# Chunked attention before two feed-forward stages: paired units in two-bank accumulators, a five-step weight conversion, and a reordered prologue

## The chip, the cores and the metric

The kernel runs on one core of one Trainium2 chip. The metric is the device time of one execution in microseconds (us); lower is better. The core has five engines, each with its own queue of instructions that it works in order: TensorE (PE in the profile, and PEld for its loads of stationary operands), VectorE (DVE), ScalarE (ACT), GpSimd (POOL) and SyncE (SP), which here only starts DMA transfers. PE writes to eight banks of PSUM; DVE and ACT read them.

## What is computed

```python
# attention: 4 batches x 8 heads, 768 positions, 64 per head; chunks of 32 queries
k_full = concat(mem_k (8), k[c_start-16 : c_end+8])      # 64 keys per chunk
a = exp(scale * (q_c @ k_full.T) - max); a = a / (sum(a) + 1e-9)
x = a @ v_full                                            # -> 3072 rows of 512
# first feed-forward stage
h = x @ w_in            # 512 x 2048
y = (relu(h) ** 2) @ w_out                                # 2048 x 512
# second stage: one of 8 experts per row, chosen by argmax(y @ w_gate)
out = gate * sigmoid(y @ w_output_gate)[e] * (relu(y @ w1[e]) @ w2[e])
```

All arrays are float32, and the result has to keep that precision.

## The kernel before

**Precision.** Most products use a 4-byte format that keeps fewer bits than float32, so each operand is split into a high part and a low part (the rest), and each product is made three times: high x high, low x high, high x low. Attention and transposes use plain float32 products. The weights of the first stage are stored as float64 (two 32-bit words per number), and are converted on the chip, tile by tile. There are 16 tiles of 1024 columns, i0, o0, i1, o1, ... (i for `w_in`, o for `w_out`). One tile takes an ACT operation that rescales the exponent (line 240, `split_w_exp`), a shift and two operations that put in the low word and the sign on DVE (lines 246 to 248, `split_w_bits`), the high part on ACT (line 260) and the low part on DVE (line 261, both in `split_w_end`). The raw tiles share three buffers (`kvp`).

**Attention.** A unit is 128 rows of one batch; there are 24, and two make a block of 256 rows. Four head pairs (`hp`) and four chunks (`c`) lie in a unit. The keys and values are laid out block-diagonally, 128 x 128 for two heads, with zeros off the diagonal, so that one product serves two heads:

```python
for hp in range(4):                      # products, lines 126-131
    for c in range(4):
        rows = slice(32 * c, 32 * c + 32)
        nc.tensor.matmul(ps[rows, hp, :], lhsT=left[:, hp, rows], rhs=right[:, hp, c, :], ...)
```

Each of these 16 products appears as two instructions in the trace. The steps of a unit are: scores on PE (`pss`), the maximum and the subtraction on DVE, exp on ACT, sum and reciprocal on DVE (`norm`), a transpose on PE (`psa`) and its copy on ACT (`at`), the product with the values on PE (`psx`), the scaling on DVE (line 196), a transpose on PE (`pst`), its high part on ACT (line 217) and its low part on DVE (line 218). For units 0 to 3 keys and values come compact and are spread over zeroed tiles by copies on DVE, ACT and GpSimd (`spread`, line 124); later units load the zeros with them (1 MB for keys, 1 MB for values).

**First stage.** For each block and each of 16 slices `f` of 128 hidden columns there is one step: `mm1` (12 products into `ph`, line 297), `relu` (r, g, gh and gl on ACT and DVE, lines 307 to 316), and `mm2` of two steps earlier (6 products into `py`, lines 326 to 328). Blocks 0 and 1 go side by side, as the weight tiles become ready; the others one after another.

**Gate and experts.** When a block's rows are done, the gate transposes them (`gate_transpose`), computes logits, chooses an expert (`gate_choose`) and counts positions (`gate_rank`), and GpSimd writes the row's number to its expert's list. Afterwards rows are gathered by expert, two tiles of 128 at a time (`Pair`) and then one at a time (`Slot`), with the expert's weights split on the way (line 564).

**What sets the order.** Instructions are issued in the order in which the program writes them. The prologue (lines 844 to 953) is written out by hand, with dummy products on PE (`keep_busy`). After it, `seq` lists the steps, n = 4, 5, ..., and `plan(n, fn)` hangs other work on a step: it comes after that step's `mm1` and before its `mm2`. Weight tile m must be ready by step 2m. `plan_unit` (line 729) places the parts of a unit, `plan_gate` (line 761) those of a gate; their comments are numbers of steps only. Unit work and gate work use the accumulators `ps_a`: two tiles of one bank each; `ps_y` holds four of one bank, `ps_h` two.

Of the kernel before, what the change touches and what calls it, by code (L numbers as in the profile page):

```python
# [8 lines left out]
F32 = mybir.dt.float32  # L9
# [8 lines left out]
P = 128  # L18
NT = 3072
D = 512  # L20
# [12 lines left out]
NCOMP = 4  # L33
SPIN = (6, 4, 3)
# [12 lines left out]
SPARE_KV = [("i6", "o6"), ("i7", "o7")]  # L47
# [3 lines left out]
def chunk_attention_relu2_moe_top1_kernel(ctx: ExitStack, tc, qt, kvc, kw, vw, w_in, w_out, wg, wexp, consts, out):  # L51
# [14 lines left out]
    ps_y = ctx.enter_context(tc.tile_pool(name="ps_y", bufs=4, space=bass.MemoryType.PSUM))  # L66
    ps_a = ctx.enter_context(tc.tile_pool(name="ps_a", bufs=2, space=bass.MemoryType.PSUM))
# [20 lines left out]
    class Unit:  # L88
        def __init__(self, u):
            self.u = u  # L90
            self.b, self.j = divmod(u, UPS)

        def load_qk(self):
            u = self.u
            self.q = qp.tile([P, 4, P], F32, tag="q", name=f"q{u}")
            nc.sync.dma_start(self.q, qt[u])
            if u < NCOMP:
                self.k, self.v = diag[u % 2]
                self.load_compact(0)
            else:  # L100
                self.k = kvp.tile([P, 4, 4, P], F32, tag="kv", name=f"k{u}")
                nc.sync.dma_start(self.k, kw[u - NCOMP])

        def load_v(self):
            u = self.u
            if u < NCOMP:
                self.load_compact(1)
            else:
                self.v = kvp.tile([P, 4, 4, P], F32, tag="kv", name=f"v{u}")
                nc.sync.dma_start(self.v, vw[u - NCOMP])  # L110


        def load_compact(self, w):
            u = self.u
            if w == 0:
                self.c = wpool.tile([P, 2, 4, 4, 64], F32, tag=SPARE_C[u], name=f"c{u}")
            nc.sync.dma_start(self.c[:, w], kvc[u, :, w])

        def spread(self, w, *copies):
            t = self.v if w else self.k  # L120
            for n, copy in enumerate(copies):
                if copy is not None:
                    rows = slice(64 * n, 64 * n + 64)
                    copy(t[rows, :, :, 64 * n : 64 * n + 64], self.c[rows, w])

        def products(self, ps, left, right):

            for hp in range(4):
                for c in range(4):
                    rows = slice(32 * c, 32 * c + 32)  # L130
                    nc.tensor.matmul(ps[rows, hp, :], lhsT=left[:, hp, rows], rhs=right[:, hp, c, :], start=True, stop=True)
# [7 lines left out]
        def scores_mm(self, pool=ps_a, tag="a"):  # L139
            self.ps = pool.tile([P, 4, P], F32, tag=tag, name=f"pss{self.u}")  # L140
            self.products(self.ps, self.q, self.k)

        def scores_max(self):
            u = self.u
            self.sc = self.ps.rearrange("p a (b k) -> p (a b) k", k=64)
            self.mx = sp_.tile([P, 8], F32, tag="mx", name=f"mx{u}")
            nc.vector.tensor_reduce(out=self.mx, in_=self.sc, axis=AX.X, op=ALU.max)

        def scores_sub(self):
            u = self.u  # L150
            self.e = ap_.tile([P, 8, 64], F32, tag="e", name=f"e{u}")
            nc.vector.tensor_tensor(
                self.e, self.sc, self.mx.unsqueeze(2).to_broadcast([P, 8, 64]), op=ALU.subtract
            )
            if self.j == 0:
                nc.vector.memset(self.e[0:32, :, 8:24], -BIG)
            if self.j == UPS - 1:
                nc.vector.memset(self.e[96:128, :, 56:64], -BIG)

        def scores_exp(self):  # L160
            nc.scalar.activation(self.e, self.e, ACTF.Exp, scale=0.125)

        def norm(self):
            u = self.u
            sm = sp_.tile([P, 8], F32, tag="sm", name=f"sm{u}")
            nc.vector.tensor_reduce(out=sm, in_=self.e, axis=AX.X, op=ALU.add)
            nc.vector.tensor_scalar_add(sm, sm, EPS)
            self.r = sp_.tile([P, 8], F32, tag="rs", name=f"rs{u}")
            nc.vector.reciprocal(self.r, sm)
# [5 lines left out]
        def transpose_a_mm(self):  # L175
            self.ps = ps_a.tile([P, 4, P], F32, tag="a", name=f"psa{self.u}")
            ef = self.e.rearrange("p a k -> p (a k)")
            for hp in range(4):
                nc.tensor.transpose(self.ps[:, hp, :], ef[:, hp * P : hp * P + P], ident)

        def transpose_a_copy(self):
            self.at = ap_.tile([P, 4, P], F32, tag="at", name=f"at{self.u}")
            nc.scalar.copy(self.at, self.ps)
# [5 lines left out]
        def av_mm(self):  # L189
            self.ps = ps_a.tile([P, 4, P], F32, tag="a", name=f"psx{self.u}")  # L190
            self.products(self.ps, self.at, self.v)
# [914 lines left out]
```

## Time and profile before

| | before |
|---|---|
| median of 3 runs | 1022.12 us (1020.71 to 1026.53) |
| the profiled execution | 1022.48 us |
| its span, first to last instruction | 1020.7 us |
| mean granted PE clock | 0.988 of full speed |
| DMA moved | 149.97 MB, mean 147 GB/s |

The span is 1.8 us shorter than the execution's own time, which has some work around it. "Busy" is time in which at least one instruction of an engine runs; instructions on PE overlap, so their durations add up to more than the busy time, and the distance from one start to the next tells what one costs. In the rows, `out<-in` names the tiles written and read without their numbers, `x32` is a count, and what stands in brackets is the idle time before the instruction with what ended it. A clock of 1.00 is PE's level of 2.4 GHz, one of 0.50 its level of 1.2 GHz.

### The profile page before, as it was taken

To read this page: it belongs to the slowest core of one execution; us is meant where nothing else is said; L and a number is where in the kernel's file an instruction comes from. 1 tells how busy PE (TensorE), PEld (TensorE's weight loads), DVE (VectorE), ACT (ScalarE), POOL (GpSimd) and SP (SyncE) were. 2 spreads that over 40 slices of the span, in tenths; PEclk is the share of its full clock that TensorE was granted. 3 is DMA by queue.
4 is the path that set the end of the run, shared out by engine and by line. 5 is a ranking of instruction groups with operands and counts; after the bars stand their busy time and mean duration, and the time that the engine had idled before them with its cause. 6 is when DMAs were issued, how large, how long until landed. Compare 5 with 4: busy or idle time off the path is not lost. (4 is left out here: it accounts for less than half of the span.)

```text
span 1020.7 us, 18715 instructions
## 1 busy us (share of the span) xinstructions
PE 985.6 (97%) x7421; PEld 866.9 (85%) x7421; DVE 620.7 (61%) x1232; ACT 470.7 (46%) x873; POOL 103.7 (10%) x99
## 2 busy tenths in 40 slices
PE   6789999999999999999999999989899999999997
PEld 3678888889898988989898989878799999888886
DVE  5799855454444545454545453566586666789995
ACT  4668533333333333333233333254344544688885
POOL 3000000000000000000000000010211222121111
PEclk9799999999999999999999999999899999999999
DMA  9256654261323223242423200094776655465531
GB/s 333 91 192 220 238 173 159 43 159 48 122 87 114 94 79 129 73 135 73 134 74 101 95 4 21 7 382 170 220 290 228 233 213 202 161 227 190 207 117 39
DMA packets 34733, 149.97 MB, mean 147 GB/s; under 512 B 8975, under 2 KB 9487, under 8 KB 20562
## 3 DMA queue, kind: packets, MB, share of 16 engines
q1 hardware_dynamic: 29394, 134.81, 38.2%
q0 software_dynamic: 5248, 13.92, 4.1%
q8 instruction: 60, 0.98, 0.4%
q14 instruction: 31, 0.25, 0.1%
HBM read 163.16 MB, written 13.61 MB: 173 GB/s over the span
## 5 line engine op out<-in xcount | busy, mean ns | idle before, releaser
L297 PE MATMUL ph<-xh,wi 128*128 128x256 f32 x1536 | 286.4, 284 | 5.6 <-DVE wi L261 2.6
L297 PEld LDWEIGHTS ph<-xh,wi 128*128 128x128 f32 x1536 | 252.5, 191 | 23.5 <-DVE wi L261 3.2
L297 PE MATMUL ph<-xl,wi 128*128 128x256 f32 x768 | 218.0, 284 | 0.1
L312 DVE TENSOR_TENSOR g<-r 128x256 f32<-128x256 f32 x168 | 71.1, 423 | 234.3 <-ACT r L307 233.8
L307 ACT ACTIVATE r<-ph 128x256 f32<-128x256 f32 x192 | 73.4, 382 | 300.1 <-PE ph L297 296.2
L326 PE MATMUL py<-wo,gh 128*128 128x512 f32 x384 | 161.5, 420 | 1.4 <-ACT wo L260 1.4
L327 PE MATMUL py<-wo,gh 128*128 128x512 f32 x384 | 151.9, 396 | 0.8 <-DVE wo L261 0.8
L328 PE MATMUL py<-wo,gl 128*128 128x512 f32 x384 | 151.4, 394 | 1.1 <-DVE gl L316 1.1
L297 PEld LDWEIGHTS ph<-xl,wi 128*128 128x128 f32 x768 | 147.0, 191 | 0.5 <-DVE xl L218 0.5
L564 DVE TENSOR_TENSOR x<-raw,x 128x1024 fp32r<-128x1024 f32 x88 | 103.1, 1221 | 8.9 <-ACT x L563 8.7
L316 DVE TENSOR_TENSOR gl<-g,gh 128x256 fp32r<-128x256 f32 x192 | 81.5, 425 | 24.1 <-ACT gh L314 1.7
L564 DVE TENSOR_TENSOR p<-raw,p 128x1024 fp32r<-128x1024 f32 x64 | 78.1, 1222 | 27.8 <-ACT p L563 27.7
L421 POOL DMA_INDIRECT listd<-ent,idx x24 | 25.5, 1060 | 643.5 <-DVE idx L419 555.2
L328 PEld LDWEIGHTS py<-wo,gl 128*128 128x128 f32 x384 | 72.4, 189 | 19.9 <-DVE gl L316 3.2
L563 ACT CAST x<-raw 128x1024 fp32r<-128x1024 f32 x88 | 87.3, 1055 | 0.0
L326 PEld LDWEIGHTS py<-wo,gh 128*128 128x128 f32 x384 | 72.6, 189 | 16.8 <-issue 4.8
L314 ACT ACTIVATE gh<-r 128x256 fp32r<-128x256 f32 x192 | 79.8, 415 | 5.3
L327 PEld LDWEIGHTS py<-wo,gh 128*128 128x128 f32 x384 | 73.0, 190 | 9.5 <-DVE wo L261 1.1
L563 ACT CAST p<-raw 128x1024 fp32r<-128x1024 f32 x64 | 66.6, 1042 | 6.5 <-DMA raw<-in_wexp 6.5
L705 PE MATMUL po<-x,ht 128*128 128x512 f32 x264 | 65.1, 397 | 0.0
L705 PEld LDWEIGHTS po<-x,ht 128*128 128x128 f32 x264 | 48.2, 188 | 9.2
L578 POOL DMA_INDIRECT out<-o,slots x27 | 33.9, 1256 | 208.8 <-ACT o L574 90.9
(227 smaller groups left out, 1439.5 us busy)
## 6 DMA issues: line engine op xcount, KB each, us to landing
raw<-in_wexp SPq DMA_DIRECT2D x82, 1024.0 KB
k<-in_kw SPq DMA_DIRECT2D x20, 1024.0 KB
v<-in_vw SPq DMA_DIRECT2D x20, 1024.0 KB
raw_i<-in_w_in SPq DMA_DIRECT2D x7, 1024.0 KB
raw_o<-in_w_out SPq DMA_DIRECT2D x7, 1024.0 KB
q<-in_qt SPq DMA_DIRECT2D x24, 256.0 KB
ydram<-y SPq DMA_DIRECT2D x24, 256.0 KB
c<-in_kvc SPq DMA_DIRECT2D x8, 512.0 KB
```

The costliest lines, as they stand in the source:

```text
L297: nc.tensor.matmul(ph, lhsT=w_in_part(w, f, k), rhs=x[:, k, :], start=(n == 0), stop=(n == 11))
L307: nc.scalar.activation(r, ph, ACTF.Relu, scale=WSCALE)
L312: nc.vector.tensor_tensor(g, r, r, op=ALU.mult)
L314: nc.scalar.activation(gh, r, ACTF.Square)
L316: nc.vector.tensor_tensor(gl, g, gh.bitcast(F32), op=ALU.subtract)
L326: nc.tensor.matmul(self.y[t], lhsT=gh[:, s], rhs=w_out_part(wh, f), start=(f == 0), stop=False)
L327: nc.tensor.matmul(self.y[t], lhsT=gh[:, s], rhs=w_out_part(wl, f), start=False, stop=False)
L328: nc.tensor.matmul(self.y[t], lhsT=gl[:, s], rhs=w_out_part(wh, f), start=False, stop=(f == NF - 1))
L563: nc.scalar.copy(w[:, 0], t)
L564: nc.vector.tensor_tensor(w[:, 1], t, w[:, 0].bitcast(F32), op=ALU.subtract)
L578: nc.gpsimd.indirect_dma_start(out=out, out_offset=bass.IndirectOffsetOnAxis(ap=slots[:, c, 0:1].bitcast(U32), axis=0), in_=self.y[t], in_ ...
L705: nc.tensor.matmul(self.po, lhsT=self.ht[:, part, f, :], rhs=w[:, wp, j * D : j * D + D], start=(f == 0 and part == 0 and wp == 0), stop=( ...
```

## The change

- **Products in row halves.** Keys and values are no longer block-diagonal. Each head is multiplied by itself: 64 rows (one half of the array), 64 columns, into one of two banks by the head's parity. All units load keys and values compact, 1 MB for both.
- **Pairs of units.** `Duo` replaces `Unit`: from block 1 on each of the steps above is made once for the two units of a block, on tiles of 1024 columns and accumulators of two banks. Block 0's units go singly in the prologue. `e`, `at` and `x` have one buffer each instead of two.
- **Accumulators.** `ps_a` is one tile of two banks, `ps_y` two of two banks. A gate's two transposes become one step, and so do a pair's; a slot's two transposes `psh` share one tile.
- **Weight conversion.** `split_w_bits` and `split_w_end` become five parts (exp, shift, or, high, low) with steps of their own, so that the exp and shift of the next tile stand ahead of the low part of this one. In the prologue only i0 is converted in halves.
- **Loads.** Queries and keys of units 0 to 3 come in one load each (rows of 6 KB), and the values of two units in one. A one-element copy on GpSimd (`hold`) into a tile makes the loads behind it wait: those of block 1 for block 0's first maximum, o0 for a reciprocal.
- **Dummies.** 41 dummy products in nine places instead of 25 in four.
- **Plan.** New steps for everything named; gates of blocks 0 to 9 come later.

```diff
-    ps_y = ... tile_pool(name="ps_y", bufs=4, space=PSUM)
-    ps_a = ... tile_pool(name="ps_a", bufs=2, space=PSUM)
+    ps_y = ... tile_pool(name="ps_y", bufs=2, space=PSUM)
+    ps_a = ... tile_pool(name="ps_a", bufs=1, space=PSUM)
...
+        def products(self, left, right, ts):
+            for i, t in enumerate(ts):
+                for hp in range(4):
+                    for par in range(2):
+                        half = slice(64 * par, 64 * par + 64)
+                        for c in range(4):
+                            rows = slice(32 * c, 32 * c + 32)
+                            n = 64 * (4 * i + hp)
+                            nc.tensor.matmul(
+                                self.ps[ts][rows, par, n : n + 64],
+                                lhsT=left[t][half, hp, rows],
+                                rhs=right[t][half, hp, c, :], start=True, stop=True)
+        def banks(self, name, ts, pool, tag):
+            self.ps[ts] = pool.tile([P, TPB, D], F32, tag=tag, ...)
...
-    plan(4, split_w_end, *tiles[3])
-    for m in range(4, 16):
-        n = 4 + (m - 4) * 3 // 2
-        plan(n, split_w, *tiles[m])
-        plan(n + 2, split_w_end, *tiles[m])
-        if m + 3 < 16:
-            plan(n, load_w, *tiles[m + 3])
+    bits = dict(zip(range(3, 16), (2, 4, 6, 8, 10, 12, 14, 15, 17, 18, 20, 21, 23)))
+    for m, n in bits.items():
+        if m > 4:
+            plan(bits[m - 1], split_w_exp, *tiles[m])
+            plan(bits[m - 1] + 1, split_w_shift, *tiles[m])
+        if m > 3:
+            plan(n, split_w_or, *tiles[m])
+            plan(n + 1, split_w_hi, *tiles[m])
+            plan(n + 1, split_w_lo, *tiles[m])
+        if m > 6:
+            plan(bits[m - 3] + 1, load_w, *tiles[m])
...
-        plan_unit(2 * b, n + 1, n + 4, n + 5, n + 7)
-        plan_unit(2 * b + 1, n + 6, n + 9, n + 10, n + 12)
+        plan_duo(b, n + 1, n + 3, n + 4, n + 6)
...
-        plan_gate(b, at[b, NF - 1] + (5, 11, 4)[min(b, 2)])
+        plan_gate(b, at[b, NF - 1] + (10, 12, 9)[min(b, 2)])
...
-        plan(last + 13 + t, pairs[0].transpose, t)
+    plan(last + 13, pairs[0].transpose)
...
-            plan(n + 5 + t, after.transpose, t)
+        plan(n + 5, after.transpose)
...
+        d0.load_first_qk(0); d0.load_first_qk(1); (ident); load_w(*i0, halves=a); d0.load_first_v()
+        keep_busy(12)
+        d0.scores_mm(u0)
+        keep_busy(4)
+        d0.scores_max(u0)
+        hold(d1.first[0], d0.mx[u0][0:1, 0, 0:1])
+        d1.load_first_qk(0); d1.load_first_qk(1); load_w(*i0, halves=b); d1.load_first_v()
+        d0.scores_sub(u0); d0.scores_mm(u1, *other); d0.scores_exp(u0); split_w_exp(*i0, a)
+        d0.transpose_a_mm(u0); d0.transpose_a_copy(u0); keep_busy(3)
+        d0.scores_max(u1); d0.scores_sub(u1); d0.scores_exp(u1); d0.norm(u0)
+        split_w_shift(*i0, a); split_w_or(*i0, a, steps=(0,))
+        d0.av_mm(u0); d0.av_scale(u0); d0.transpose_a_mm(u1, *other); d0.transpose_a_copy(u1); keep_busy(3)
+        d0.norm(u1); hold(o0t, d0.r[u1]); load_w(*o0); load_w(*i1); (consts)
...
+        d1.scores_mm(); split_w_exp(*i0, b); b0.mm1_products(0); keep_busy(8)
+        d1.scores_max(); d1.scores_sub(); b0.relu(0); d1.scores_exp()
+        split_w_shift(*i0, b); split_w_or(*i0, b); ...; split_w_lo(*i0, b); keep_busy(3)
+        d1.av_mm(); split_w_exp(*o0); b0.mm1_products(1); d1.av_scale()
+        split_w_shift(*o0); split_w_or(*o0, steps=(0,)); d1.transpose_x_mm(); d1.transpose_x_hi()
+        b0.relu(1); keep_busy(4); d1.transpose_x_lo(); split_w_or(*o0, steps=(1,))
+        b1.mm1_products(0); load_w(*o1); split_w_exp(*i1); split_w_hi(*o0); split_w_shift(*i1); split_w_lo(*o0)
+        b1.relu(0); split_w_or(*i1); load_w(*i2); b1.mm1_products(1); split_w_exp(*o1); b1.relu(1)
+        split_w_hi(*i1); split_w_shift(*o1); split_w_lo(*i1); b0.mm2(0); split_w_or(*o1)
+        load_w(*o2); split_w_exp(*i2); b0.mm2(1); split_w_hi(*o1); split_w_shift(*i2); split_w_lo(*o1)
```

(Lines of the prologue are joined with semicolons here.) The pair's gate, `Block.mm2`, `Pair.mm2` and `Slot` take their accumulators in tiles of two banks, and `yt` uses the tag of the converted weights; what they compute is unchanged.

## Rows read from the trace of the kernel before

**Rows 1.** The page: busy us, share of the span and instructions of each engine.

```profile
PE 985.6 (97%) x7421; PEld 866.9 (85%) x7421; DVE 620.7 (61%) x1232; ACT 470.7 (46%) x873; POOL 103.7 (10%) x99
```

**Rows 2.** Windows: each engine's busy us and instructions, PE clock, DMA share, GB/s.

```profile
5.00:68.70 63.70, 45.40 (x439) 35.07 (x436) 46.49 (x76) 37.89 (x63) 6.63 (x10) 0.87 0.57 208
68.70:117.00 48.30, 47.22 (x294) 41.32 (x295) 47.61 (x57) 37.97 (x68) 0.00 (x0) 1.00 0.65 232
150.00:640.00 490.00, 490.00 (x4231) 438.54 (x4230) 231.97 (x645) 159.33 (x390) 20.50 (x20) 1.00 0.29 91
```

**Rows 3.** Timeline of PE at 300 us: start, duration, line, operation, count.

```profile
302.46 0.40 PE L297 MATMUL ph<-xh,wi 128*128 128x256 f32 x2
...
305.28 0.40 PE L297 MATMUL ph<-xh,wi 128*128 128x256 f32 x2
...
310.92 0.40 PE L297 MATMUL ph<-xh,wi 128*128 128x256 f32 x2
...
314.96 0.40 PE L297 MATMUL ph<-xh,wi 128*128 128x256 f32 x2
```

**Rows 4.** Timeline of PE, prologue: sets of 32 small products.

```profile
13.99 1.94 PE L131 MATMUL pss<-diag_i,q 128*32 128x128 f32 x32
15.70 1.18 PE L131 MATMUL psx<-diag_o,at 128*32 128x128 f32 x32
...
19.89 1.08 PE L131 MATMUL psx<-diag_o,at 128*32 128x128 f32 x32
20.79 1.06 PE L131 MATMUL pss<-diag_i,q 128*32 128x128 f32 x32
```

**Rows 5.** Window of one such set; the clock stands third last.

```profile
13.99:15.70 1.71, 1.71 (x34) 1.59 (x36) 0.00 (x0) 1.58 (x3) 0.66 (x1) 0.50 1.02 407
```

**Rows 6.** Timelines of ACT, DVE and PE, prologue.

```profile
5.58 1.04 ACT L124 COPY diag_i<-c 64x1024 f32<-64x1024 f32 x1 [3.54 <-DMA c<-in_kvc]
...
7.82 0.69 DVE L147 TENSOR_REDUCE mx<-pss 128x8 f32<-128x512 f32 x1 [1.49 <-PE pss L131]
...
68.69 0.39 PE L297 MATMUL ph<-xh,wi 128*128 128x256 f32 x1 [2.30 <-DVE wi L261]
```

**Rows 7.** Groups on DVE, 5 to 68.7 us: busy us, mean ns, idle before.

```profile
L316 DVE TENSOR_TENSOR gl<-g,gh 128x256 fp32r<-128x256 f32 x8 | 3.4, 421 | 1.7 <-ACT gh L314 1.7
...
L147 DVE TENSOR_REDUCE mx<-pss 128x8 f32<-128x512 f32 x4 | 2.7, 684 | 5.6 <-PE pss L131 5.6
...
L124 DVE COPY diag_i<-c 64x1024 f32<-64x1024 f32 x3 | 2.1, 705 | 4.2 <-DMA c<-in_kvc 4.2
L246 DVE TENSOR_SCALAR ws_i<-ws_i 128x512 int32<-128x512 int32 x4 | 1.7, 418 | 0.0
...
L248 DVE SCALAR_TENSOR_TENSOR ws_o<-raw_o,ws_o 128x1024 int32<-128x1024 int32 x2 | 2.5, 1225 | 0.1
...
L246 DVE TENSOR_SCALAR ws_o<-ws_o 128x1024 int32<-128x1024 int32 x2 | 1.4, 692 | 0.3 <-ACT ws_o L240 0.3
```

**Rows 8.** Windows of the first 15 us; the last two columns are DMA.

```profile
0.00:5.00 5.00, 3.99 (x10) 1.49 (x11) 1.82 (x2) 1.28 (x1) 4.29 (x10) 1.00 0.57 170
5.00:10.00 5.00, 3.57 (x42) 1.47 (x39) 2.30 (x4) 2.36 (x3) 2.18 (x2) 1.00 0.94 326
10.00:15.00 5.00, 2.05 (x24) 1.66 (x28) 0.69 (x1) 3.34 (x5) 1.03 (x1) 0.75 0.99 348
```

**Rows 9.** Groups on DVE, whole span: one operation of a block's rank.

```profile
L415 DVE TENSOR_TENSOR pb<-psr,base 128x8 f32<-128x8 f32 x24 | 3.9, 162 | 0.4
```

**Rows 10.** Timelines of GpSimd and PE: gathers and the first gathered rows.

```profile
665.25 0.97 POOL L542 DMA_INDIRECT ys<-ydram,slots  x1 [7.51 <-PE py L328]
666.53 0.96 POOL L542 DMA_INDIRECT ys<-ydram,slots  x1 [0.30 <-issue]
...
672.95 0.63 PE L553 MATMUL psz<-cst,ys 128*128 128x128 f32 x4 [3.20 <-DMA ys<-ydram,slots]
...
726.79 1.08 PE L553 MATMUL psz<-cst,ys 128*128 128x128 f32 x4 [4.31 <-DMA ys<-ydram,slots]
```

More of the change, by code (lines that the diff above doesn't have):

```diff
@@ L32 @@
 BIG = 1.0e30
-NCOMP = 4
-SPIN = (6, 4, 3)
+EARLY = 4
+BOTH = (0, 1)
 F2B = F2 // P
@@ L85, in chunk_attention_relu2_moe_top1_kernel @@
     wh, wl = {}, {}
[L88 to L131, printed above, removed]
@@ L137, in scores, with scores_mm @@
             self.scores_exp()
[L139 to L151, printed above, removed]
+        def scores_mm(self, ts=BOTH, pool=ps_a, tag="a"):
+            self.banks("pss", ts, pool, tag)
+            self.products(self.q, self.k, ts)
@@ L155, in scores_sub @@
[L155 to L166, printed above, removed]
+                self.e[:, self.heads(ts)].rearrange("p a b k -> p b a k"),
@@ L226, in load_w @@
         t = raw[kind, g].rearrange("p n two -> p (n two)")
+        if not issue:
+            return t
         src = (w_in if kind == "i" else w_out)[g].bitcast(I32)
@@ L321, in mm2 @@
             if f == 0:
-                self.y = [ps_y.tile([P, D], F32, tag="y", name=f"py{b}_{t}") for t in range(TPB)]
+                y = ps_y.tile([P, TPB, D], F32, tag="y", name=f"py{b}")
+                self.y = [y[:, t] for t in range(TPB)]
             gh, gl = self.g.pop(f)
@@ L624, in mm2 @@
             if f == 0:
-                self.po = [ps_y.tile([P, D], F32, tag="y", name=f"po{p}_{t}") for t in range(TPB)]
+                po = ps_y.tile([P, TPB, D], F32, tag="y", name=f"po{p}")
+                self.po = [po[:, t] for t in range(TPB)]
             gh, gl = self.g.pop(f)
@@ L713, in chunk_attention_relu2_moe_top1_kernel @@
     tiles = [(kind, g) for g in range(8) for kind in "io"]
-    units = {u: Unit(u) for u in range(NU)}
+    duos = {b: Duo(b) for b in range(NB)}
     blocks = {b: Block(b) for b in range(NB)}
@@ new lines, in chunk_attention_relu2_moe_top1_kernel @@
+        d0.norm(u0)
+        split_w_shift(*i0, a)
+        split_w_or(*i0, a, steps=(0,))
+        d0.av_mm(u0)
+        d0.av_scale(u0)
+        d0.transpose_a_mm(u1, *other)
+        d0.transpose_a_copy(u1)
+        keep_busy(3)
+        d0.norm(u1)
+        o0t = load_w(*o0, issue=False)
+        hold(o0t.bitcast(F32), d0.r[u1][0:1, 0, 0:1])
+        load_w(*o0)
+        load_w(*i1)
+        nc.sync.dma_start(cst[:, P:], consts[:, P:])
+        d0.av_mm(u1, *other)
+        d0.av_scale(u1)
```

482 lines of the change are left out of this document (267 added, 215 removed).

## The prediction

> **What bounds the kernel now.** I read the page's busy line first [rows 1]: TensorE (PE) is busy for 97% of the span, VectorE (DVE) for 61%. An average over the span hides stages, so the table of windows comes next [rows 2]. From 150 to 640 us PE is busy for all 490 us at full clock, while DVE works 232 us: there only work taken off PE shortens the time. From 5.0 to 68.7 us it is the other way: PE works 45.4 of 63.7 us, DVE 46.5, and DVE waits for 17.2 us. There a chain through all engines sets the end. From 68.7 to 117 us both are nearly full (47.2 and 47.6 of 48.3 us).
>
> The timeline of PE shows what attention costs in the full stage [rows 3]. A plain step of the planner (12 products of the first matmul, 6 of the second) lasts 305.28 - 302.46 = 2.82 us. The step into which the scores of one unit are put lasts 314.96 - 310.92 = 4.04 us. So one unit's set of 32 small products costs 1.22 us of PE time. Where two such sets stand back to back [rows 4], the second starts 20.79 - 19.89 = 0.90 us after the first: 0.90 us is the products, 28 ns each, and 1.22 - 0.90 = 0.32 us is paid for entering and leaving. At a granted clock of 0.50 the same 32 products take 15.70 - 13.99 = 1.71 us [rows 4, 5], nearly twice as long: their price follows TensorE's clock.
>
> The prologue's timeline has three marks [rows 6]: at 5.58 us DVE may begin to spread the first keys, at 7.82 it takes the first maximum, and at 68.69 PE goes on in step 8 after 2.30 us of waiting for DVE's last operation on weight tile i2. From there PE hardly waits.
>
> **The change, part by part.**
>
> *Products in halves.* The products no longer multiply through zeros. Each 128-row, 128-column product becomes two of 64 rows and 64 columns, on the two row halves of the array, with outputs in two banks; two units are done in one set. A set has 128 instructions instead of 2 x 32 = 64, and 24 units become 12 pairs. Ten pairs (blocks 2 to 11) lie in or beside the full stage, with two sets each: 20 places. Before, a place costs 2 x 1.22 = 2.44 us. After, entering and leaving is paid once (0.32), and the products lie between two bounds. Below: half the columns and twice the tiles at work, so a quarter of 28 ns each: 128 x 7 = 0.90 us, in all 1.22. Above: each instruction costs what one costs now: 128 x 28 = 3.6, in all 3.9. In between: columns set the price, but the two halves of rows don't run at once: 128 x 14 = 1.8, in all 2.1. The trace speaks for columns: the price nearly doubled with the half clock [rows 4, 5], and four column tiles now run side by side. I take the lower end plus 0.2 us for a sequencer that must now issue four times as fast: 1.42 us. 20 x (2.44 - 1.42) = **20 us less**; ends 24 less and 30 more.
>
> A page of the Trainium skill speaks against this: "TensorE: Matmul & The Clock Gate", section "Back-to-back issue gap", gives a product of 1 to 64 columns a floor of about 25 ns. By it a place would cost about 3.5 us, some 1.1 more than now. No row of this trace has products this narrow in a long set, so neither is shown.
>
> *Prologue.* I count DVE's work up to i2's end, since DVE is what step 8 waits for. Before: 46.5 us between 5.0 and 68.7 [rows 2]. Gone are four spreading copies (4 x 0.7: 2.8 us) [rows 7]. Units 2 and 3 are paired: five operations of 1024 elements (about 1.22) for ten of 512 (0.69): 0.8 less. Tiles o0 and i1 are converted whole, not in halves: for each 0.42 + 3 x 0.69 twice is 5.0, against 0.69 + 3 x 1.22 = 4.4: together 1.2 less. Of tile o2 only the shift (0.69) still stands ahead of i2's end, not all three bit operations (3.1): 2.4 less. That leaves 46.5 - 7.2 = 39.3 us.
>
> When can it start? The first queries and keys are the same 0.79 MB as before, in one load instead of two, and need no spreading. Before, they had landed at 5.58 [rows 6], and 7.82 - 6.62 = 1.2 us lay between the end of spreading (5.58 + 1.04, ACT's half) and the first maximum. So that comes at about 6.5. Without a wait, i2 would be done at 6.5 + 39.3 = 45.8 us, 23 us earlier than now. There will be waits. The values of units 0 and 1 are fifth in the queue, behind 2.1 MB; at the rates of [rows 8] (170 GB/s over 5 us is 0.85 MB, then 2.5 MB by 10 us and 4.2 by 15) they land near 12 us, when DVE, with 5 us of work after its first maximum, has run dry for about 1 us. At each hand-over PE, ScalarE (ACT), DVE of the chains it waits again, but the new order puts a conversion step into most of these gaps (shift and first "or" of i0 ahead of the scaling of unit 0; halves of o0 around the second pair). I take half of the 17.2 us of waiting as left: i2 done at 45.8 + 8.6 = 54.4. PE comes a little later: from i1's end to step 8 it needs four steps, 11.3 us, while DVE does i2 9.6 us after i1 (two operations of o1, its low part, two shifts, two of i2, its low part, two gl of 0.42). Step 8 then stands at 54.4 + 1.7 = 56. **Gain 13 us**. With all waiting left it is 5, with 3 us left 18.
>
> The dummies rise from 25 to 41, in PE's gaps; DVE's chain hides them, and they cost something only where it is early. The holds are one-element copies on GpSimd; behind the first one SP holds only the loads of units 2 and 3, half of i0 and their values (3.1 MB, needed from about 17 us on).
>
> Does the gain last until the end? Afterwards a tile is needed every two steps (5.64 us) and costs DVE 4.4 us and two gl of 0.42, 5.2 in all. DVE keeps pace with 0.4 us to spare. If that cover were gone, PE would wait for tiles, as at 68.69.
>
> *One accumulator of two banks in place of two of one bank.* Every use now waits until the last one is read. In a block the pair uses it in steps 1, 3, 4 and 6 and the gate later, with 2.82 us or more between; the reads (1.22 at most, behind a gl) fit. I find three places where they don't. Block 0's rank and block 1's transposes fall on the same step, 43: the transposes wait for four reads of 0.16 us [rows 9] behind g and gl: 2 us. In pair 0, rank waits behind the transposed rows' low part, which stands after the gate's chain and a weight split on DVE: 1 us, bounds 0 and 2.8 (one plain step). And pair transposes are made at once, so the first two wait for both gathers: these were already late by 3.20 and 4.31 us, and the second gather of a pair is issued 1.28 us after the first [rows 10]; four transposes (0.44) of that are useful: 0.85 each, 1.7. **Cost 5 us** (1 to 9).
>
> *The rest* I cost at nothing: longer rows and half the bytes for keys and values of blocks 2 on (DMA is busy 29% from 150 to 640 [rows 2]); gates in one transpose set (the same eight instructions); fewer, wider operations on DVE and ACT there, idle for half the stage. With the cover of PE gone they would count, as in the last stage, but there the number of operations is unchanged.
>
> **Sum.** The profiled execution took 1022.48 us: - 20 - 13 + 5 = 994.5. The median of the runs is 0.36 lower, so **994 us**.
>
> **The rivals.**
> *Row halves don't overlap* (0.18): a place costs 2.1 us, gain 20 x 0.34 = 7. 1022 - 7 - 13 + 5 = 1007. For it: no row shows two row halves at work.
> *The prologue stays bound by its chain* (0.08): gain 5, so 1022 - 20 - 5 + 5 = 1002. This is the case in which reordering and holding do not do what they are for: values land late, and DVE waits as before.
> *Products priced by the piece* (0.13), the one that ends slower: a place costs 3.9 us, 1.5 more than now, 30 us in all; 1022 + 30 - 13 + 5 = 1044. It decides as soon as the other parts' 8 us are eaten up: 0.4 us more a place than now, 2.84 us, 20 ns a product. For it: 28 ns is what every set shows. Against it: the price changed with the clock. The floor that the Trainium skill gives in "TensorE: Matmul & The Clock Gate" (section "Back-to-back issue gap") would make it 1022 + 22 - 13 + 5 = 1036.
> *All parts nearly cancel* (0.05): products at 18 ns, prologue 5.
>
> **How the numbers follow.** My forecast has 0.56, with its own range 984 to 1005 (products 24 to 16 less, prologue 18 to 8, cost 1 to 8; not all at one end). With the two milder rivals the range is 982 to 1017: it leaves out the priced pieces and a little on the fast side. A measurement of this kernel tells 0.5%, 5 us, from no change. Faster by more: 0.56 + 0.18 + 0.08, less a little of their upper ends, 0.79; the same 0.07; slower 0.14.
>
> **What would show it.** Timeline of PE around a block's scores: a set of 128 products that lasts about 1.2 us is right; 2 us means halves that don't overlap; 3.5 us means pieces. The two sets of a block should take 2.8 us of PE together, against 4.9 now. Step 8 near 56 us and about 9 us of DVE waiting ahead of it would bear out the prologue. Idle time of PE ahead of the transposes at step 43 and of the first gathered rows shows the costs. I am wrong if sets last over 2.8 us, or if step 8 stays past 63 us.

## The result, and the profile after

The changed kernel takes 1012.12 us (median of 4 runs, 1010.41 to 1013.84); beside it the kernel before took 1021.8. The ratio is 0.9896 (95%: 0.9859 to 0.9934): 10 us less, where 28 were forecast. The profiled execution took 1013.84 us, with a span of 1011.7, so 8.6 us less than the profiled one of before.

The page's busy line and three windows (columns: window, its length, busy us and instructions of each engine, granted clock of PE, DMA share, GB/s):

```profile
PE 975.9 (96%) x8973; PEld 862.7 (85%) x8973; DVE 607.6 (60%) x1133; ACT 458.6 (45%) x808; POOL 97.5 (10%) x92
```

```profile
5.00:55.40 50.40, 41.80 (x710) 31.45 (x708) 39.46 (x56) 27.10 (x46) 2.07 (x7) 0.93 0.67 254
...
68.70:117.00 48.30, 46.43 (x413) 41.49 (x412) 44.12 (x58) 33.17 (x60) 0.00 (x0) 1.00 0.60 210
150.00:640.00 490.00, 484.20 (x5269) 436.88 (x5268) 223.35 (x588) 158.07 (x353) 20.03 (x20) 0.99 0.15 54
```

Against [rows 1, 2]: PE's share fell by a point, and from 150 to 640 us, where it had been busy for all 490 us, it now stands still for 5.8 us, with a clock below 1.00. The change has put holes into the one stage that had none.

PE's timeline around a block's scores (start us, length, engine, line, operation, tiles, count), which answers to [rows 3, 4]:

```profile
309.50 0.40 PE L345 MATMUL ph<-xh,wi 128*128 128x256 f32 x2
...
311.02 1.51 PE L134 MATMUL pss<-kv,q 64*32 64x64 f32 x128
...
313.96 0.40 PE L345 MATMUL ph<-xh,wi 128*128 128x256 f32 x2
```

The step lasts 4.46 us, 1.64 more than the plain 2.82. And step 8, which answers to the last row of [rows 6], now starts at 55.38 us with no idle time ahead of it:

```profile
55.38 0.40 PE L345 MATMUL ph<-xh,wi 128*128 128x256 f32 x2
```

So neither sign named in the forecast for "I am wrong" came (sets over 2.8 us, step 8 past 63 us), and still the sum is off by 18 us. To find where, I laid the starts of all steps (the first `mm1` product of each) of both traces side by side:

| step | before, us | after, us | ahead by |
|---|---|---|---|
| 9 | 71.48 | 58.20 | 13.3 |
| 33 | 148.53 | 133.40 | 15.1 |
| 34 | 152.57 | 144.08 | 8.5 |
| 43 | 185.28 | 175.30 | 10.0 |
| 44 | 188.53 | 182.85 | 5.7 |
| 50 | 208.24 | 207.34 | 0.9 |
| 53 | 218.01 | 220.72 | -2.7 |
| 176 | 628.26 | 619.20 | 9.1 |
| 247 | 851.82 | 841.10 | 10.7 |

The whole gain of the prologue is lost between steps 33 and 53. After that each block regains 1.27 us (52.09 in place of 53.36 a block). The loss sits in three places. PE's waits name them (waited for; us in all, times, longest; `issue` stands for a wait for nothing that the profile shows):

```profile
PE pss L134 <- DMA kv<-in_kv: 4.2, 2, 3.5
PE ph L345 <- ACT r L355: 3.9, 2, 3.0
PE pss L134 <- issue: 2.7, 1, 2.7
...
PE psz L602 <- DMA ys<-ydram,slots: 2.4, 2, 1.2
PE psy L397 <- DVE pb L465: 2.2, 1, 2.2
...
PE psr L457 <- DVE zl L607: 1.4, 1, 1.4
...
PE pss L134 <- DMA q<-in_qt: 0.9, 1, 0.9
```

**Step 33.** The scores of block 3 wait for their queries and then for half of their keys:

```profile
135.92 0.85 PE L134 MATMUL pss<-kv,q 64*32 64x64 f32 x64 [0.93 <-DMA q<-in_qt]
140.25 1.17 PE L134 MATMUL pss<-kv,q 64*32 64x64 f32 x64 [3.48 <-DMA kv<-in_kv]
```

SP's timeline says why. Its queue is in order, and the two stores of block 0, which wait for DVE's y, stand ahead of these loads. PE wants the queries at 135.92 - 0.93 = 134.99 us and the keys at 140.25 - 3.48 = 136.77; they are issued 2.5 and 3.3 us earlier:

```profile
131.50 0.92 SPq L388 DMA_DIRECT2D ydram<-y  x2
132.51 0.91 SPq L117 DMA_DIRECT2D q<-in_qt  x2
133.51 0.38 SPq L122 DMA_DIRECT2D kv<-in_kv  x1
```

**Step 43.** Block 1's transposes wait for DVE's reads of block 0's rank, the place that the forecast named:

```profile
179.15 1.35 PE L397 MATMUL psy<-cst,y 128*128 128x128 f32 x8 [2.20 <-DVE pb L465]
```

**Steps 49 to 53.** PE stops six products before the end of a set, and the profile shows nothing that it waits for:

```profile
199.79 1.46 PE L134 MATMUL pss<-kv,q 64*32 64x64 f32 x122
203.98 0.70 PE L134 MATMUL pss<-kv,q 64*32 64x64 f32 x6 [2.73 <-issue]
```

Behind each of these three stops the clock is lower. The windows of a stop and of what follows it:

```profile
136.00:140.30 4.30, 0.82 (x71) 0.69 (x75) 0.42 (x1) 0.00 (x0) 0.00 (x0) 0.83 0.62 248
140.30:146.00 5.70, 5.70 (x81) 4.95 (x82) 3.30 (x4) 1.06 (x1) 0.00 (x0) 0.53 0.00 0
...
179.20:183.00 3.80, 3.80 (x15) 3.22 (x16) 0.26 (x2) 1.01 (x1) 1.12 (x1) 0.58 0.01 0
201.30:204.00 2.70, 0.02 (x1) 0.00 (x0) 0.00 (x0) 0.00 (x0) 0.00 (x0) 0.94 0.06 6
204.00:210.50 6.50, 6.50 (x26) 5.42 (x26) 4.12 (x6) 1.42 (x2) 0.96 (x1) 0.50 0.00 0
```

After 2.2 to 3.5 us without work PE goes on at a granted clock of 0.50 to 0.58 (mostly the level of 1.2 GHz) for some 4 to 6.5 us, and pays for the stop a second time.

A fourth loss is hidden inside a gain: from step 187 to 193 the changed kernel takes 26.6 us and the kernel before 22.4. There PE waits for ACT's r (the 3.0 us above) and for gathered rows (the 2.4 us).

### The profile page after: what moved, and what is told of

It reads as the page before. It is cut to its first block, busy times and chain, and to the rows that moved or that the text cites. A ratio compares the mean times of both kernels' runs of the same rounds, so it can differ in the third digit from the quotient of the medians.

```text
span 1011.7 us, 21585 instructions
## 1 busy us (share of the span) xinstructions
PE 975.9 (96%) x8973; PEld 862.7 (85%) x8973; DVE 607.6 (60%) x1133; ACT 458.6 (45%) x808; POOL 97.5 (10%) x92
## 5 line engine op out<-in xcount | busy, mean ns | idle before, releaser
L375 PEld LDWEIGHTS py<-wo,gh 128*128 128x128 f32 x384 | 73.6, 192 | 13.1 <-issue 2.5
L628 POOL DMA_INDIRECT out<-o,slots x27 | 36.3, 1344 | 215.6 <-DVE o L622 98.0
```

Source lines behind the costliest of these rows:

```text
L375: nc.tensor.matmul(self.y[t], lhsT=gh[:, s], rhs=w_out_part(wh, f), start=(f == 0), stop=False)
L628: nc.gpsimd.indirect_dma_start(out=out, out_offset=bass.IndirectOffsetOnAxis(ap=slots[:, c, 0:1].bitcast(U32), axis=0), in_=self.y[t], in_ ...
```

## The experiments

The theory: the parts do what the forecast said, and the 18 us are lost in these single stops and the half clock behind them. The rival: time is lost a little everywhere, to dearer products and the single accumulator. The kernel before ran beside each group; its medians lay between 1020.1 and 1023.4 us.

### Two waits taken away

`again` is the changed kernel unaltered. `load_early`:

```diff
+            early = 5 if b == 2 else 0
-            plan(x + 1, after.load_kv, 0)
+            plan(x + 1 - early, after.load_kv, 0)
...
-            plan(x + 3, after.load_kv, 1)
+            plan(x + 3 - (4 if early else 0), after.load_kv, 1)
```

(The queries' loads, between the two, are moved as the first.) `gate_late`:

```diff
-        plan_gate(b, at[b, NF - 1] + (10, 12, 9)[min(b, 2)])
+        plan_gate(b, at[b, NF - 1] + (10, 13, 9)[min(b, 2)])
```

`both` has the two edits.

> The changed kernel once more, nothing altered, as the base for the runs beside it. The theory: the forecast's two gains are there (step 8 near 55.4 us; 12 places with less PE time), and the missing 18 us are lost in four single stops of PE between steps 33 and 53, each followed by a stretch at half clock. Three of them are waits for data and must recur to 0.1 us: pss for DMA kv and q (4.4 us in step 33), psy for DVE pb (2.2 us in step 43), ph for ACT r (3.0 us at 661 us). The fourth, 2.7 us of 'issue' inside the scores of step 49, is open: if it stands at the same product again (the 122nd), it belongs to the order of the instructions; if it is gone or elsewhere, it is chance, and the time is then some 5 us shorter (about 1009 in place of 1013.8). The rival: the time is lost a little everywhere (dearer products, the single accumulator); then the stops move about while the time stays at 1012.

> Block 3's pair of units has its queries, keys and values loaded five to four steps earlier, ahead of block 0's two stores in SP's queue; nothing else is changed. The theory: both waits of step 33 (0.9 and 3.5 us) go, and the half clock behind them with them, so step 34 comes 6.6 us earlier and the kernel takes 6.6 us less than the changed one, 1005.5. The rival without the clock: only the waits themselves go, 4.4 us, 1007.7. The rival that the loads are late for another reason (the transfer itself, its buffer): no wait goes, 1012.

> Block 1's gate starts one step later, so that its transposes don't fall on the step of block 0's rank; nothing else is changed. The theory: the wait of 2.2 us in step 43 goes, and the half clock behind it: step 44 comes 4.3 us earlier, 1007.8. The rival without the clock: 2.2 us, 1009.9. The rival that the single accumulator makes the next use wait in its place (rank at step 48 against the scores at 49): nothing is gained, 1012.

> Both of these edits together. The theory: the gains add up, 6.6 + 4.3 = 10.9 us, 1001.2, and the ratio to the kernel before is 0.980. Waits alone: 6.6 us, 1005.5. If time is lost everywhere, about 1012. If the stop inside the scores of step 49 comes from where blocks of instructions fall, it should stay, since the order of PE's instructions up to there is nearly the same.

| kernel | median, us | ratio to before (95%) | step 33 to 34 | 43 to 44 | 49 to 53 |
|---|---|---|---|---|---|
| changed | 1012.1 | 0.9896 (0.9859 to 0.9934) | 10.7 | 7.5 | 22.4 |
| `again` | 1012.0 | 0.9899 (0.9862 to 0.9937) | 10.5 | 7.7 | 22.3 |
| `load_early` | 1004.5 | 0.9839 (0.9799 to 0.9878) | 4.5 | 6.1 | 22.6 |
| `gate_late` | 1005.0 | 0.9831 (0.9794 to 0.9867) | 10.4 | 3.0 | 18.6 |
| `both` | 998.9 | 0.9781 (0.9740 to 0.9823) | 4.5 | 3.0 | 15.4 |

Each stop goes with its edit, and with the wait goes the half clock: 6.2 us of step 33 for 4.4 us of waiting. The medians fell by 7.6, 7.0 and 13.1 us, against 6.6, 4.3 and 10.9. The rival of small losses everywhere explains none of this fall, for a steady block lasts 52.09 us in the changed kernel and in `both`. It isn't out as a whole: the forecast took 2 x 1.02 = 2.04 us off a block and the trace shows 1.27, which is some 8 us over ten blocks.

The clock doesn't fall behind every stop. In `load_early` the same 2.20 us of step 43 are followed by a clock of 1.00, and the step lasts 6.1 us in place of 7.5:

```profile
172.67 1.06 PE L397 MATMUL psy<-cst,y 128*128 128x128 f32 x8 [2.20 <-DVE pb L465]
```

```profile
172.80:176.60 3.80, 3.80 (x30) 3.40 (x33) 0.18 (x2) 1.02 (x2) 1.12 (x1) 1.00 0.01 0
```

The stop inside the scores of step 49 stood after the 122nd product in `again` too, and after the 121st in `load_early`; in `gate_late` it shrank to two gaps of 0.35 and 0.44 us, with another of 1.78 three steps later, and in `both` it was gone. From step 49 to 53 `both` is 7 us shorter than the changed kernel (15.4 for 22.4), which neither edit was made for. This stop is the part that stayed open.

### What PE stops for in a set

A set of 128 products is 256 instructions with its weight loads, in 1.5 us; a plain step issues 36 in 2.82 us. The page counts the transfers that bring instructions (queue: packets, MB, share of time), first of the kernel before, then of the changed one:

```profile
q8 instruction: 60, 0.98, 0.4%
```

```profile
q8 instruction: 72, 1.18, 0.5%
```

These are packets of 16 KB, one for every 250 of PE's 18,023 instructions in the trace. Most take 0.9 to 1.4 us, but a few 2 to 3; in the changed kernel such ones stand at 188.2 (2.83 us) and 202.1 (2.48), around the stop. `split49` puts half of that one set into the next step, `shift32` and `shift64` put dummies ahead of it, and `narrow` makes each product of three sets as two of half the columns (the lines are shortened):

```diff
+    plan(46, dummies, 32)      # shift32; 64 in shift64
...
-            plan(s, d.scores)
+            plan(s, d.scores_first)       # split49, block 4: unit 0's 64 products
+            plan(s + 1, d.scores_rest)    # unit 1's, then maximum, subtraction, exp
...
+                            for j in range(0, 64, 32):    # narrow, blocks 6 to 8
+                                matmul(ps[rows, par, n + j : n + j + 32], lhsT=..., rhs=right[t][half, hp, c, j : j + 32])
```

> The changed kernel, with one set alone made shorter: of block 4's scores 64 products stand in step 49 and 64 in step 50 (its transposes, values and loads follow one step later). The theory of the supply of instructions: a set of 128 products (256 instructions with the weight loads) in 1.5 us comes to the end of what has been fetched whenever a fetch just before it took over 2 us; with half the burst PE does not stop in steps 49 to 53, no half clock follows, and step 54 comes 6 to 7 us earlier, less 0.3 us for entering a set twice: 1005.5. The rival: the slow fetch stops PE wherever it stands, in the next step too: 1012.

> The changed kernel with 32 dummy products (64 instructions, about 2 us) put into step 46, ahead of the set of step 49 in which PE stopped after 122 of 128 products in two profiles of the changed kernel, and after 121 in the one with the loads moved ahead. If the stop belongs to a position in the stream of PE's instructions (a block of 256 that has not come yet), it moves 32 products ahead, to the 90th. If it belongs to the place in the program (the end of that set, the loads or the stores then under way), it stays at about the 122nd. If it is chance, it is gone. Step 47 starts 2 us later than in the changed kernel in every case, by the dummies.

> The same with 64 dummies (128 instructions, about 4 us). By the position in the stream the stop moves 64 products ahead, to the 58th; by the place in the program it stays at about the 122nd.

> The kernel with both edits; in the scores of blocks 6, 7 and 8 each product of 64 columns is made as two of 32 (256 products in a set for 128, the same numbers). If columns set the price: the step with the scores stays at 4.47 us. If each product has a price of its own of about 10 ns (issue): 256 x 10.3 ns + 0.32 us is 2.96 us over the plain step, 5.78 us. In between, part of the price is the piece's. A set of 512 instructions may also stop for want of them, which is then told apart by its gap.

`split49` took 1007.0 us, ratio 0.9857 (0.9820 to 0.9894). No stop is left in the set of step 49, and step 54 comes 5.8 us earlier; but the next set stops after 115 products for 0.95 us. So the theory has the larger part and the rival a part too. `shift32` (one run, 1001.7 us) has no stop there at all: 32 dummies, 2 us of PE, brought step 54 forward by 6.2 us. (Another 7 us of its lower time lie in steps 187 to 193, which take 19.6 us in place of 26.6 and which the dummies don't touch.) `shift64` (one run, 1006.8) stops in the next set instead, after 111 and 114 products:

```profile
215.21 1.33 PE L134 MATMUL psx<-kv,at 64*32 64x64 f32 x111
217.09 0.30 PE L134 MATMUL psx<-kv,at 64*32 64x64 f32 x3 [0.56 <-issue]
218.22 0.40 PE L134 MATMUL psx<-kv,at 64*32 64x64 f32 x14 [0.83 <-issue]
```

None of the forecasts of a place (90th, 58th product, or the 122nd again) was met, so the place in the program alone is out as a cause. That the stop is gone, as in `shift32`, was the forecast for chance; but chance alone doesn't fit a stop after the 122nd, 122nd and 121st product in three profiles. `narrow` (one run, 1006.8 us) shows the same from the other side: with 512 instructions in a row two of its three sets stop for about 2 us, the third for 0.5, though the packets around the first took 0.88 and 1.02 us:

```profile
296.96 1.07 PE L135 MATMUL pss<-kv,q 64*32 64x32 f32 x88 [2.05 <-issue]
...
348.58 2.34 PE L135 MATMUL pss<-kv,q 64*32 64x32 f32 x219
352.78 0.55 PE L135 MATMUL pss<-kv,q 64*32 64x32 f32 x37 [1.86 <-issue]
```

To see what these stops share I numbered PE's instructions (products and weight loads, in order of start) and listed, for all sixteen profiles with the change, the gaps of 0.3 us and more between 60 and 640 us that the profile puts down to "issue". Of 27, 17 stand at a number 193 above a multiple of 256: eight profiles have one at 4801, three at 3521, and single ones at 6849, 7105, 8385 and 10689 and two at 9665. In `nofill`, `best2` and `best3` 29 products are missing ahead of it, so 4801 is another product there (in a first matmul, not in a second), and still PE stops at 4801. That is a position in the stream, the same one within each 256 instructions, which is about one packet. The other ten don't fit: they stand in or around two sets (4276 to 4405, 4884 and 4890), and the one that cost most, after the 122nd product, is among them, at 4398. The packets' own times say what ends the stops. 17 of the 27 end 1.9 to 2.5 us after the start of an instruction packet, though such packets start only every 12 us or so. Among the 17 are the three of 2.7 to 3.4 us after the 121st or 122nd product, and 14 of those at 193 above. Of the rest, three of 1.8 to 2.1 us end 4.4 to 4.9 us after a packet's start, and seven are under 0.9 us. So PE waited for its own instructions in most of these stops, all of 2.2 us and more among them; why mostly in this block and seldom in the seven that follow, whose sets are as long, stays open.

### What a product costs

`narrow` also prices the product. In the rows above 219 products of 32 columns took 2.34 us and 37 took 0.55, so (2.34 - 0.55) / 182 = 9.8 ns each; of 64 columns 128 took 1.51 us and 64 took 0.85 (first row of step 33), so 10.3 ns each. Half the columns, the same price: the third set of `narrow`, with a stop of 0.51 us, makes its step 6.41 us long, where 5.78 were expected of a price by the piece and 4.47 of one by columns. A piece is a product with its weight load; `narrow` doubles both, so which of the two sets the price isn't told apart. `par` changes the order only:

```diff
-                for hp in range(4):
-                    for par in range(2):
+                for par in range(2):
+                    for hp in range(4):
```

> The kernel with the loads moved ahead and the gate one step later, and the products of a set in another order: all 16 of one row half, then all 16 of the other, so that neighbours no longer lie on both halves. The same products are made. The theory that neighbours on two row halves run side by side: without that the price goes from 10 to 14 ns a product, a set from 1.65 to 2.1 us over the plain step, 20 sets, 9 us: 1008. The rival that products are paced by their issue, one by one, whatever tiles they use: sets stay at 1.65 us, 999.

```profile
403.41 1.78 PE L134 MATMUL pss<-kv,q 64*32 64x64 f32 x128
414.65 1.73 PE L134 MATMUL psx<-kv,at 64*32 64x64 f32 x128
```

A set costs 1.86 to 1.90 us over the plain step in place of 1.60 to 1.65, about half of what was expected if halves ceased to overlap; over 20 sets 5 us. The median, 1000.9 us (ratio 0.9780, 0.9734 to 0.9826), doesn't tell it from `both`; the steps do. So neighbours on two row halves do help, but what is left at best is a price by the piece. The Trainium skill ("TensorE: Matmul & The Clock Gate", section "Back-to-back issue gap") has such a price, about 25 ns for 1 to 64 columns; an estimate by it is 3.2 us for 128 products. These sets took 1.5: the kind of price agrees, the number doesn't.

### The prologue's dummies and holds

`nofill` is `both` without the 29 dummies behind the first twelve; `nohold` is `both` with this edit:

```diff
         def hold(tile_, until):
-            nc.gpsimd.tensor_copy(tile_[0:1, 0:1], until)
+            pass
```

> The kernel with both edits, without the 29 dummies after the first twelve. If the dummies hold the clock up: PE's own work between 20 and 43 us, 15 us at a granted clock of 0.93, goes at 0.50 for the most part, about half of it lies on the chain, step 8 comes 5 to 7 us later and the kernel takes 1005. If DVE's chain hides them, as the forecast had it: step 8 stays at 57 us within 1 us, 999.

> The kernel with both edits, without the three one-element copies on GpSimd that hold loads back (two in the prologue's first part): all first loads are issued as SP comes to them. If holding is what brings the first values early: 3.1 MB more share the 16 DMA engines before the values of units 0 and 1 (now landed at 13 us), these land at about 17 us, and step 8 comes 3 to 4 us later than 57.0, the kernel takes 1002 to 1003. If order alone does it: step 8 within 1 us of 57.0, 999.

| kernel | median, us | ratio (95%) | step 4, us | step 8, us | step 187 to 193 | granted clock, 20 to 43 us |
|---|---|---|---|---|---|---|
| `both` | 998.9 | 0.9781 (0.9740 to 0.9823) | 43.0 | 57.0 | 27.2 | 0.93 |
| `nofill` | 995.0 | 0.9750 (0.9706 to 0.9794) | 45.2 | 57.7 | 19.3 | 0.70 |
| `nohold` (2 runs) | 993.8 | 0.9714 (0.9666 to 0.9761) | 43.3 | 55.8 | 23.8 | 0.93 |

The dummies (41 in the change, in eight places and not nine) do hold the clock up, and step 4 shows what it buys. PE's wait there for DVE's low part of tile i1 ends 2.2 us later without them, first in `both`, then in `nofill`:

```profile
44.22 0.39 PE L345 MATMUL ph<-xh,wi 128*128 128x256 f32 x1 [0.87 <-DVE wi L309]
```

```profile
46.44 0.38 PE L345 MATMUL ph<-xh,wi 128*128 128x256 f32 x1 [0.87 <-DVE wi L309]
```

DVE's chain does set this step, but it passes through PE's products, which are slower at the lower clock (a set of 128 ahead of it takes 2.05 us in `nofill` and 1.48 in `both`). At step 8 only 0.7 us of the 2.2 is left, because in `both` PE goes on at a clock of 0.52 from 45.1 to 48.6 us and loses 1.5 us, and in `nofill` it doesn't. One profile of each is too little to go by, but there are sixteen: step 4 starts at 41.8 to 44.2 us in the thirteen with the 29 dummies and at 45.2, 46.8 and 47.3 in the three without (`nofill`, `best3`, `best2`); step 8 at 54.7 to 58.3 and at 57.7, 59.3 and 59.8, in the mean 3 us later. So the dummies gain some 3 us. That `nofill` still ends ahead of `both` comes from steps 187 to 193, 8 us shorter in it, where the two programs are the same. That stretch lasts from 18.9 to 27.2 us in the sixteen profiles; what sets it was not looked into, and it can blur a comparison of medians.

The holds show no such gain. The first values landed at 13.2 us with them and at 13.3 without:

```profile
13.20 0.85 PE L134 MATMUL psx<-v,at 64*32 64x64 f32 x64 [3.34 <-DMA v<-in_vv]
```

```profile
13.30 1.17 PE L134 MATMUL psx<-v,at 64*32 64x64 f32 x64 [3.11 <-DMA v<-in_vv]
```

That the two are faster than `both` is not shown; the intervals overlap. What is left for the 13 us of the prologue, besides the dummies, is the compact keys, the pairing and the new order of the conversion; none of these was taken away by itself.

### The causes put together

`best` is `both` with two more edits. `best2` is `best` without the 29 dummies and with pair 0's weight splits one step later; `best3` is `best2` with the logits where the change has them; `best4` is `best3` with the dummies and without the holds.

```diff
-    plan(last + 13, pairs[0].transpose)
+    plan(last + 14, pairs[0].transpose)
...
+        if 2 <= b < NB - 3:
+            n += 11                       # best, best2: logits, choice, rank
...
-            ps = ps_a.tile([P, TPB, D], F32, tag="a", name=f"psl{b}")[:, 0]
+            ps = ps_h.tile([P, D], F32, tag="h", name=f"psl{b}")      # best, best2
...
-    for u, i in enumerate((10, 11, 11, 12, 13, 14, 15)):
+    for u, i in enumerate((11, 12, 12, 13, 14, 15, 15)):              # best2 to best4
```

> The kernel with both edits, and two more: for blocks 2 to 8 the gate's logits stand in the step of a pair's values, 11 steps later, with a bank of the first matmul's accumulators (before the change they stood beside a unit's values, too); and pair 0's transposes stand one step later. The theory that entering and leaving a set costs 0.32 us once, whatever stands in it: the step with the logits, 3.58 us now, falls to the plain 2.82 and the step with the values grows by 0.41 to 0.45, 0.32 us a block, 2.2 us in all. The transposes' step later: the two waits for gathered rows (5.2 us in the kernel with both edits) become about 2.4 us, and less half clock follows, 3 us. Together 993.5. The rival that these move the wait elsewhere (rank behind the pair's transposed rows, step 192 for the low part): 997 to 999.

> The kernel with both edits, the logits beside the values, pair 0's transposes one step later, without the 29 later dummies, and with pair 0's weight splits one step later each (in the kernel with both edits ScalarE waits 5.6 us for a raw weight at 636 to 641 us with the ReLU of the next step behind it, and PE waits 1.6 us). Dummies: -1; splits: -1.5 to -2.5; against the 994.1 of the kernel with the four edits: 991. The rival: the logits beside a set (288 instructions in one step) leave a stop for instructions somewhere, as at 462 us there (3.4 us and its tail), 994.

> The same without the move of the logits: each of the blocks 2 to 8 gives back 0.16 us, 1.1 in all, and there is no step with 288 instructions in a row: 992 if stops don't matter, 989 if the move of the logits caused one.

> What has paid so far, put together: loads of block 3's pair moved ahead, block 1's gate a step later, no holds, all dummies kept, pair 0's transposes and weight splits one step later, the logits left where the change puts them. Without the holds the kernel with both edits took 993.8; its stretch from step 187 to 193 lasted 23.9 us, against 18.9 to 21.7 in the two kernels with transposes and splits later: 4 us less, 990, ratio 0.969. If the stops for instructions fall badly (one costs 5 to 7 us with its half clock), 995.

`best` took 994.1 us, ratio 0.9737 (0.9699 to 0.9775), as forecast, though not by the parts forecast. The step with the logits fell from 3.58 to 2.82 us, but the one with the values rose by 0.57, so a block gains 0.16 us, not 0.32. The waits for pair 0's gathered rows fell from 5.2 to 0.6 us; that the later transposes did it is not shown, for these waits are 0.3 us in `nofill` without that edit and 3.5 in `best4` with it. And one block has a new stop, behind a set and the logits in one step (288 instructions):

```profile
465.50 0.40 PE L375 MATMUL py<-wo,gh 128*128 128x512 f32 x1 [3.35 <-issue]
```

The other three were misses: 997.7 (0.9751, 0.9701 to 0.9801), 998.9 (0.9757, 0.9718 to 0.9795) and 994.9 (0.9732, 0.9704 to 0.9760) for 991, 989 to 992 and 990. The later splits did what was expected (step 188 lasts 2.8 us, not 3.6 to 6.0). But `best2` and `best3` lack the dummies: their step 8 comes at 59.8 and 59.3 us, that of `best` at 55.9, a loss of 3.5 to 4 us where a gain of 1 was expected. And each of the three has a stop at number 4801, here of `best4`, 2.07 us, with a clock of 0.65 in the 4.7 us behind it:

```profile
207.26 0.50 PE L377 MATMUL py<-wo,gl 128*128 128x512 f32 x1 [2.07 <-issue]
```

So `both`, `nofill`, `nohold` and these four end between 993.8 and 998.9 us, against 1012 for the changed kernel and 1022 for the one before; which of them is best can't be told from these runs.

## Why the prediction was right and wrong

**The prologue was right, with some luck.** Step 8 was put at 56 us and came at 55.38. From the first maximum (6.91 us, forecast 6.5) to the end of tile i2 (53.88, forecast 54.4) DVE's work was counted as 39.3 us and the waiting left as 8.6; it works 37.97 of 46.97 us and waits 9.0. PE's last wait ahead of step 8, for i1, ends at 44.12, and four plain steps of 2.82 later it is 55.4, as counted:

```profile
6.91:53.88 46.97, 38.37 (x635) 29.23 (x634) 37.97 (x54) 25.64 (x43) 2.07 (x7) 0.93 0.65 243
```

```profile
44.12 0.39 PE L345 MATMUL ph<-xh,wi 128*128 128x256 f32 x1 [0.88 <-DVE wi L309]
```

That the gain would last to the end of the conversion was right too. The dummies were costed at nothing, hidden by DVE's chain; they gain some 3 us that the count didn't have, so the place of step 8 was met in part by luck. (One bound was added up wrongly: with all waiting left the gain is 68.69 - 45.8 - 17.2 - 1.7 = 4 us by the forecast's own terms, not 5.)

**The products had the right place, and the wrong mechanism.** A place was forecast at 1.42 us and measured 1.60 to 1.65, from 2.44: 20 x 0.8 = 16 us in place of 20. The step that failed is "half the columns and twice the tiles at work, so a quarter of 28 ns". The price isn't one of columns any more: at 64 and at 32 columns it is about 10 ns a piece. The rival of the piece had the right kind of price, but took its size, 28 ns, from the wider products of before (128 rows, 128 columns); why those cost more a piece was not tested. What [rows 4, 5] showed of the clock misled me: at a granted clock of 0.50 a product of the new kind takes (2.05 - 1.17) / 64 = 13.8 ns against 10.3, a third more and not twice. These are two sets in `nofill`, timeline of PE, both at a clock of 0.50 from start to end:

```profile
12.93 1.17 PE L134 MATMUL psx<-v,at 64*32 64x64 f32 x64 [3.24 <-DMA v<-in_vv]
...
27.74 2.05 PE L134 MATMUL psx<-v,at 64*32 64x64 f32 x128 [1.10 <-ACT at L213]
```

**"The same eight instructions" failed.** That was said of the gate's transposes; the whole gate was costed at nothing, its logits too. Before, they stood beside a unit's values and shared its 0.32 us of entering and leaving; their step was 0.41 us longer for them. Now they stand alone at 3.58 - 2.82 = 0.76. That is 0.35 us a block, 3.5 in all, and the rest of why a block gains 1.27 us and not 2.04.

**The single accumulator.** Step 43 was named, with 2 us; the wait was 2.20, the cost 4.3, for this stop had a second price in half clock that no term of the sum had. Pair 0's rank waits 1.4 us for 1. The gathers were to cost 1.7; in fact waits on them fell from 7.5 us [rows 10] to 2.4 (4.4 in `again`), and from step 176 to 247 the changed kernel gains 1.6 us: 4.2 lost from 187 to 193, 5.8 gained behind that.

**What the sum didn't have.** "Longer rows and half the bytes for keys and values", costed at nothing, went by bytes and DMA's busy share. The new plan had also put block 3's loads behind block 0's stores in SP's queue, one step ahead of their use: 6.2 us. I asked of the holds what stands behind them in SP's queue, and not of the stores. And the supply of instructions was no term at all: 7 us in steps 49 to 53.

With the measured sizes the sum closes: -15.1 (to step 33) - 9 x 1.27 (blocks) + 6.2 + 4.3 + 7.0 (three stops) - 1.6 (pairs) + 1.7 (the gain of 10.7 at step 247 ends as 9.0 on the span; that stage was not looked into) = -8.9, against -8.6 for the two profiled executions. That it closes tests little, since most of its terms are differences between the same traces.

## What to carry to other kernels

A forecast's signs of failure must cover what isn't in the sum: neither of mine came, though two thirds of the forecast gain were missing, and 13 us of that stood at two places that no term named. When steps are re-planned, write down for each load what now stands ahead of it in its queue and how many us before its use it is issued, and count for a stop of 2 to 4 us on a busy TensorE the slower clock that can follow it, which here made the three stops cost 1.4 to 2 times their length. Compare a stretch across all profiles that share its program before a difference in it is put down to an edit. Work cut into many small instructions is priced by the piece, and in bursts of hundreds it can wait for its own instructions.

## What the runs showed of the hardware that was not expected

- Products of 64 rows by 32 on eight tiles of the array cost, with their weight loads, 9.8 to 10.3 ns each, whether they have 32 or 64 columns; in `par`, where neighbours lie on the same row half, a set of 128 costs 0.25 us more.
- PE stopped for 0.45 to 3.35 us with nothing else in the profile to wait for, 17 times at a number 193 above a multiple of 256, in eleven profiles. 14 of these stops ended 2.2 to 2.5 us after the start of an instruction packet. In one run 32 dummies ahead of a stop brought step 54 forward by 6 us.
- Some of the 16 KB packets of instructions took 2.0 to 3.5 us where most took about 1. In all sixteen profiles one of these came around PE's 4000th instruction, at 177 to 189 us.
- After a stop the clock fell in most cases but not in all: behind 2.20 us in step 43 it was 0.58 in the changed kernel and 1.00 in `load_early`, and behind the 3.35 us of `best` it was 1.00.
